# Start of a fused attention and MLP kernel: loads spread over two queues, and a new order of steps up to the third slot

## The chip, the cores and the metric

The kernel runs on one core of a Trainium2 chip. The core has a matrix engine (TensorE, in the profile PE, with its weight loads as PEld), a vector engine (VectorE, DVE), an engine for functions (ScalarE, ACT), a general engine (GpSimd, POOL) and an engine that mostly issues transfers (SyncE, SP). ScalarE can issue transfers too. All transfers are carried by 16 DMA engines. Each engine works through its own list of instructions in order, and waits where an operand isn't there yet.

The metric is the device time of one execution in microseconds (us). Before the change it was 173.32 us, the median of three runs (173.28 to 174.05).

## The reference

There are 2048 tokens of width 512. The result is the input, plus a linear attention of its layer norm, plus an MLP of the same layer norm. Cut to what matters (32 heads of 16):

```python
xn = layernorm(x)
q, k, v = split_heads(xn @ wqkv)
phi(t) = concat(softmax(t @ w_phi), softmax(-(t @ w_phi)))       # per head, 16 -> 32
kv = phi(k)^T @ v ;  z = sum over tokens of phi(k)
attn = (phi(q) @ kv) / (phi(q) . z + 1e-6) @ wo
h = xn @ w1 + b1                                                 # width 1792
mlp = (h * tanh(softplus(h))) @ w2                               # Mish
out = x + attn + mlp
```

## The kernel before, in words

Tokens lie in 16 tiles of 128, and four tiles form a group. A *slot* is a group whose keys (slots 0 to 3) or queries (slots 4 to 7) go through the feature map. The feature weights w_phi are folded into the key and query weights, so that a slot's logits come from one projection.

The order of the work is written out by hand in the table `STEPS`. Each entry is a step, and every engine gets its instructions in the order of the steps. `@` gives the PSUM bank (0 to 5) that a step writes. A letter at the end says who copies a result out of PSUM: `a` ScalarE, `v` VectorE. A step may write a bank only when its last content has been copied out. The steps that matter here:

- `AW n` is a dummy matmul of n columns, which keeps TensorE busy before there is data.
- `LS i`, `RS i`, `AZ i`: statistics of token tile i (VectorE), its reciprocal root (two tiny ScalarE instructions with `a`, two GpSimd ones with `p`), and the normalised tile (VectorE). `TP i @b` turns it on TensorE with four transposes, and `TC i` copies it out into `xnT`.
- The key weights `wkp` are needed turned for the fold. Half of them (row blocks 0 and 1) comes in naturally, is turned on TensorE (`TW kt`) and copied out (`TK kt`) into `wT`. The other half (row blocks 2 and 3) is turned by a transposing DMA. `WB` builds the block-diagonal feature weights `Wbd` from `wsrc`. `F0 kt` folds a row block with four matmuls, and `FD kt` copies it back into `wkp`.
- `LP` makes the logits of tiles 0 and 1 in eight matmuls (line 244). With `i` they alternate between the two tiles, one row block after the other.
- `V t` and `VC t`: values of a tile (four matmuls) and their copy. `L s i` and `LC s i`: logits of tile i of slot s (four matmuls) and their copy. `WL i` are logits of slot 1 that go to a wide PSUM tile. `H u` and `M u`: four matmuls of the first MLP layer, and Mish on ScalarE.
- `E s`, `X s k`, `S s k`, `R s k`, `N s k`, `A s k`: subtraction of extremes (VectorE), exponentials (ScalarE), sums (VectorE), reciprocals (ScalarE with `a`), normalisation (VectorE), accumulation into kv (TensorE, 16 matmuls).
- `LN g` and `AP g k`: statistics of a later group and its normalised halves, turned by DMA. `F`, `FC`, `FT`: the fold of the query weights. `PB` and `CB` bring the bias b1 into its layout.

ScalarE's functions lie in two table sets, one for Mish and one for exponential and logarithm. A step that needs the other set loads it first (line 139, `ACT_TABLE_LOAD`).

Nothing plans the order at run time: the table and the order of the loads (lines 517 to 533) set it. SP issues nearly all loads, ScalarE issues two small ones ahead of its first table load.

Of the kernel before, what the change touches and what calls it, by code (L numbers as in the profile page):

```python
# [59 lines left out]


# [1 line left out]
def kernel(  # L63
# [19 lines left out]
    FT = F // P  # L83
# [10 lines left out]
    b1_v = B_b1.rearrange("(f p) -> f p", p=P)  # L94
# [12 lines left out]
    x_sb = persist.tile([P, NT, D], BF16, name="x_sb")  # L107
# [118 lines left out]
    def project(w, t, pp):  # L226

        for kt in range(KT):
            nc.tensor.matmul(  # L229
                pp, lhsT=xnT[:, t, kt, :], rhs=w(kt),  # L230
                start=(kt == 0), stop=(kt == KT - 1),
            )
        return pp
# [292 lines left out]
    nc.scalar.dma_start(b1b[:], b1_v[:, :])  # L526
    with nc.allow_non_contiguous_dma(reason="tiny w_phi load"):
        nc.scalar.dma_start(wsrc[:], wphi_v)
# [191 lines left out]
```

## Time and profile before

| | |
|---|---|
| median of three runs | 173.32 us (173.28 to 174.05) |
| the profiled execution's own time | 173.45 us |
| its span in the profile | 171.7 us |
| PE busy | 166.9 us, 97% |
| DVE busy | 142.0 us, 83% |
| ACT busy | 124.4 us, 72% |
| HBM read and written | 7.10 MB and 2.10 MB |

The span is what lies between the first and the last instruction of the profiled execution. The 1.75 us around it belong to the execution's time. A row of the timeline gives the start and the length in us, the engine, the line, and what is written from what. `x8` means that eight instructions are merged, and in brackets stands how long the engine had been idle and what ended that. Instructions of VectorE and ScalarE overlap a little with the next one of the same engine, so the distance between two starts is often shorter than the length shown. A row of the windows gives the length of the stretch and then, engine by engine, busy time and count (PE, PEld, DVE, ACT, POOL), the granted clock of TensorE, the DMA engines' share and GB/s.

### The profile page before, as it was taken

How to read it: one execution, taken by the hardware profiler on the slowest of the kernel's cores; microseconds unless marked ns; L12 is line 12 of the kernel's file. 1: busy time of each engine (PE TensorE's matmuls, PEld its weight loads, DVE VectorE, ACT ScalarE, POOL GpSimd, SP SyncE). 2: the span in 40 equal slices, each digit the busy share in tenths (PEclk: the TensorE clock that was granted, in tenths of full speed). 3: DMA queues.
4: the chain of work that ended last, by engine and by line, in shares of the span. 5: the costliest groups of instructions: out<-in, count | busy, mean ns of one | idle time of the engine just before them, and what ended most of it. 6: DMA issues, size and time to landing. Idle time of an engine off the chain costs nothing.

```text
span 171.7 us, 2732 instructions
## 1 busy us (share of the span) xinstructions
PE 166.9 (97%) x1035; PEld 82.3 (48%) x1050; DVE 142.0 (83%) x221; ACT 124.4 (72%) x203; POOL 7.4 (4%) x21
## 2 busy tenths in 40 slices
PE   8899999999999999999999999999999999999993
PEld 3654444444444544454445644544444444554452
DVE  2968999989999999439989999899799998884333
ACT  3765999998999999799978989968272792432200
POOL 4021230200000000000000000000000000000000
PEclk9999999999999999999999999999999999999999
DMA  5997195184299100000000293309445628778741
GB/s 127 287 376 256 21 215 101 32 154 94 39 218 357 59 4 0 0 0 4 0 0 0 51 113 84 61 18 130 102 110 109 148 61 189 156 160 207 91 124 61
DMA packets 46297, 18.55 MB, mean 108 GB/s; under 512 B 38092, under 2 KB 46284, under 8 KB 46284
## 3 DMA queue, kind: packets, MB, share of 16 engines
q1 hardware_dynamic: 45584, 18.26, 46.4%
q10 hardware_dynamic: 700, 0.12, 0.4%
q8 instruction: 8, 0.13, 0.3%
q14 instruction: 5, 0.04, 0.1%
HBM read 7.10 MB, written 2.10 MB: 54 GB/s over the span
## 4 chain that ended last, share of the span: by engine, by line
PE 94%; DVE 2%; DMA 1%; issue 1%; ACT 0%
PE ph L263 28%; PE po L497 28%; PE pl L229 14%; PE pv L229 8%; PE po L504 8%; PE pnd L452 2%; PE pkv L421 2%; DMA x_sb<-in_A_x_dram 1%; PE pwide L229 1%; PE pl L244 1%; DVE stats L165 1%; PE ptr L609 1%; DVE wkp L160 0%; PE pfold L151 0%; DVE xn L176 0%
## 5 line engine op out<-in xcount | busy, mean ns | idle before, releaser
L497 PE MATMUL po<-w_sb,acts 128*128 128x512 bf16 (+2 forms) x232 | 50.2, 366 | 0.3
L263 PE MATMUL ph<-xnT,w_sb 128*128 128x512 bf16 x224 | 50.3, 379 | 0.0
L274 ACT ACTIVATE acts<-ph,b1f 128x512 bf16<-128x512 f32 x56 | 35.8, 698 | 3.1 <-PE ph L263 3.0
L340 DVE TENSOR_REDUCE s<-e 128x128 f32<-128x2048 bf16 x16 | 36.3, 2276 | 0.5 <-ACT e L323 0.5
L263 PEld LDWEIGHTS <-w_sb 128*128 128x128 bf16 x224 | 21.6, 98 | 25.7 <-issue 0.2
L497 PEld LDWEIGHTS <-acts 128*128 128x128 bf16 x238 | 22.1, 98 | 23.6
L323 ACT ACTIVATE e<-e 128x2048 bf16<-128x2048 bf16 x16 | 30.4, 1914 | 0.0
L229 PEld LDWEIGHTS <-xnT 128*128 128x128 bf16 x184 | 17.6, 98 | 20.4 <-issue 0.2
L287 ACT CAST p_sb<-pl 128x512 bf16<-128x512 f32 x26 | 14.8, 590 | 4.9 <-PE pl L229 4.8
L511 DVE TENSOR_TENSOR x_sb<-po,x_sb 128x512 bf16<-128x512 f32 (+2 forms) x17 | 11.0, 657 | 8.3 <-PE po L504 8.3
L229 PE MATMUL pl<-wqk,xnT 128*128 128x512 bf16 x64 | 15.6, 379 | 0.0
L229 PE MATMUL pv<-wv,xnT 128*128 128x512 bf16 x63 | 15.4, 379 | 0.1
L504 PE MATMUL po<-wqk,xnT 128*128 128x512 bf16 (+2 forms) x65 | 15.0, 366 | 0.2
L467 ACT COPY ds<-pnd 128x32 f32<-128x32 f32 x16 | 2.9, 183 | 16.5 <-PE pnd L452 16.5
L307 DVE TENSOR_TENSOR e<-p_sb,m 128x2048 bf16<-128x2048 bf16 x8 | 9.8, 1226 | 5.4 <-PE pkv L421 5.1
L165 DVE BATCH_NORM_STATS2 stats<-x_sb 128x6 f32<-128x512 bf16 x16 | 10.1, 680 | 4.3 <-DMA x_sb<-in_A_x_dram 4.3
L139 ACT ACT_TABLE_LOAD x10 | 12.8, 1283 | 0.2
L298 DVE TENSOR_TENSOR m<-m 128x512 bf16<-128x512 bf16 (+1 forms) x32 | 11.5, 359 | 1.1
L229 PE MATMUL pl<-wkp,xnT 128*128 128x512 bf16 x45 | 11.8, 379 | 0.2
L298 DVE TENSOR_TENSOR m<-p_sb 128x1024 bf16<-128x1024 bf16 x16 | 10.9, 682 | 0.3 <-ACT p_sb L287 0.3
L307 DVE TENSOR_TENSOR e<-m,p_sb 128x2048 bf16<-128x2048 bf16 x8 | 9.8, 1225 | 0.3
L374 DVE TENSOR_TENSOR e<-e,r 128x2048 bf16<-128x2048 bf16 x8 | 9.6, 1217 | 0.5 <-ACT r L349 0.5
(71 smaller groups left out, 129.0 us busy)
## 6 DMA issues: line engine op xcount, KB each, us to landing
w_sb<-in_B_w_dram SPq DMA_DIRECT2D x4, 896.0 KB, 8.3
out_dram<-x_sb SPq DMA_DIRECT2D x15, 128.0 KB, 1.9
x_sb<-in_A_x_dram SPq DMA_DIRECT2D x3, 512.0 KB, 8.2
wv<-in_A_wqkv_dram SPq DMA_DIRECT2D x1, 512.0 KB, 4.9
wqk<-in_A_wo_dram SPq DMA_DIRECT2D x1, 512.0 KB, 4.0
x_sb<-in_A_x_dram SPq DMA_DIRECT2D x2, 128.0 KB, 2.3
wkp<-in_A_wqkv_dram SPq DMA_DIRECT2D x1, 256.0 KB, 3.3
x_sb<-in_A_x_dram SPq DMA_DIRECT2D x1, 256.0 KB, 4.1
```

The lines of the kernel that those rows point to most:

```text
L139: nc.scalar.preload_act_table_set(name)
L165: nc.vector.bn_stats(stats[:, i, :], xs[:, i, :])
L229: nc.tensor.matmul(pp, lhsT=xnT[:, t, kt, :], rhs=w(kt), start=(kt == 0), stop=(kt == KT - 1),)
L263: nc.tensor.matmul(ph_of[u][:], lhsT=w1_sb[:, kt, f * P : (f + 1) * P], rhs=xnT[:, g * TPG : (g + 1) * TPG, kt, :], start=(kt == 0), stop= ...
L274: nc.scalar.activation(acts[:, f, g * 512 : (g + 1) * 512], ph_of.pop(u)[:], ACT.Mish, bias=b1f[:, f : f + 1])
L287: copy(p_of[s][:, i, :], pl_of.pop((s, i)))
L298: nc.vector.tensor_tensor(out=m[:], in0=src[:, :, 0:half], in1=src[:, :, half : 2 * half], op=op)
L307: nc.vector.tensor_tensor(out=e_of[s][:].rearrange("p t j l c -> p (t j) l c")[:, :, pl, :].rearrange("p t (c e o) -> p t c e o", e=8, o=2 ...
L323: nc.scalar.activation(v, v, ACT.Exp)
L340: nc.vector.reduce_sum(t[:], pair(s, k).rearrange("p t j l (c e) -> p (t j l c) e", e=16), axis=AX.X)
L497: nc.tensor.matmul(po_of[t, c.stop][:, c], lhsT=acts[:, f, t * P : (t + 1) * P], rhs=w2_sb[:, f, c], start=(f == 0), stop=False,)
L504: nc.tensor.matmul(po_of[t, c.stop][:, c], lhsT=oT_of[t // 2][:, t % 2 * 4 + j, :], rhs=wo_sb[:, j, c], start=False, stop=(j == 3),)
```

## The change

Five loads at the start are moved. SP keeps tile 0, then at once the transposing DMA of half of the key weights, tiles 2 and 3, and now the bias b1, ahead of the rest as before. ScalarE's queue gets the feature weights first, then the natural half of the key weights, then tile 1. Line numbers behind it fall by two.

The table `STEPS` is new from its start to the step `H 38` (logits of slots 0 to 3 and the first of slot 4), and from there on it is the same but for bank numbers. There are 13 dummies with 4480 columns in place of 15 with 4928. `WL 2` now comes ahead of `WL 1`, for which the allocation of the wide tile is made on first use.

```diff
-AW 256; AW 512; AW 128; AW 512; AW 256; AW 256; AW 512; AW 256; LS 0; AW 512; AW 512; LS 1; AW 256;
...
+AW 64; AW 512; LS 0; RS 0 a; AW 512; AW 128; AW 512; AW 512; AW 512; AZ 0; LS 1; AW 512; AW 512; AW
+256; AW 64; TW 0 @0; TW 1 @3; TK 0 a; WB v; TK 1 v; TP 0 @1; AW 256; RS 1 a; F0 0 @4; AZ 1; AW 128;
...
-    for t in range(2):
-        nc.sync.dma_start(x_sb[:, t, :], x_v[:, t, :])
-
-
+    nc.sync.dma_start(x_sb[:, 0, :], x_v[:, 0, :])
     wT_of = {0: lnp.tile([P, 4, 512], BF16, name="wT", tag="xn")}
-    nc.sync.dma_start(wkp[:, 0:2, :], wqkv_v[:, 0:2, D : 2 * D])
     nc.sync.dma_start_transpose(
         out=wT_of[0][:, :, 2 * P : 4 * P], in_=A_wqkv[2 * P : 4 * P, D : 2 * D]
     )
-    nc.scalar.dma_start(b1b[:], b1_v[:, :])
     with nc.allow_non_contiguous_dma(reason="tiny w_phi load"):
         nc.scalar.dma_start(wsrc[:], wphi_v)
+    nc.scalar.dma_start(wkp[:, 0:2, :], wqkv_v[:, 0:2, D : 2 * D])
+    nc.scalar.dma_start(x_sb[:, 1, :], x_v[:, 1, :])
     nc.sync.dma_start(x_sb[:, 2:4, :], x_v[:, 2:4, :])
+    nc.sync.dma_start(b1b[:], b1_v[:, :])
     nc.sync.dma_start(wv[:], wqkv_v[:, :, 2 * D : 3 * D])
...
     def wide(i):
-        if i == 1:
+        if not wide_of:
```

VectorE's list at the start, before. BN_STATS and BN_AGGR are a tile's statistics (`LS`), xn is a normalised tile (`AZ`), Wbd is `WB`, wT is `TK`, xnT is `TC`:

```order
L165 BN_STATS stats<-x_sb 128x6
L167 BN_AGGR mv<-stats 128x2
L165 BN_STATS stats<-x_sb 128x6
L167 BN_AGGR mv<-stats 128x2
L176 TENSOR_SCALAR xn<-x_sb,mv,rstd 128x512 x2
L565 TENSOR_TENSOR Wbd<-block,wsrc 128x512
L621 COPY wT<-ptw 128x4x128 x2
L668 CAST b1f<-pb 128x14
L627 COPY xnT<-ptr 128x512
L160 CAST wkp<-pfold 128x512
```

The same place now:

```order
L165 BN_STATS stats<-x_sb 128x6
L167 BN_AGGR mv<-stats 128x2
L176 TENSOR_SCALAR xn<-x_sb,mv,rstd 128x512
L165 BN_STATS stats<-x_sb 128x6
L167 BN_AGGR mv<-stats 128x2
L563 TENSOR_TENSOR Wbd<-block,wsrc 128x512
L619 COPY wT<-ptw 128x4x128
L176 TENSOR_SCALAR xn<-x_sb,mv,rstd 128x512
L625 COPY xnT<-ptr 128x512 x2
```

Tile 1's statistics moved behind tile 0's normalised tile, both copies to xnT moved to VectorE, and one wT copy and the fold's copy left it.

ScalarE's list at the start, before (rstd is `RS`, wkp from pfold is `FD`):

```order
L526 DMA b1b<-in_B_b_dram 14x128
L528 DMA wsrc<-in_A_w_phi_dram 128x4x16
L535 ACT_TABLE_LOAD
L594 ACTIVATE rstd<-mv,eps 128x1
L595 ACTIVATE rstd<-rstd 128x1
L594 ACTIVATE rstd<-mv,eps 128x1
L595 ACTIVATE rstd<-rstd 128x1
L627 COPY xnT<-ptr 128x512
L160 CAST wkp<-pfold 128x512 x3
```

The same place now:

```order
L523 DMA wsrc<-in_A_w_phi_dram 128x4x16
L524 DMA wkp<-in_A_wqkv_dram 128x2x512
L525 DMA x_sb<-in_A_x_dram 128x512
L533 ACT_TABLE_LOAD
L592 ACTIVATE rstd<-mv,eps 128x1
L593 ACTIVATE rstd<-rstd 128x1
L619 COPY wT<-ptw 128x4x128
L592 ACTIVATE rstd<-mv,eps 128x1
L593 ACTIVATE rstd<-rstd 128x1
L160 CAST wkp<-pfold 128x512 x4
```

Two large loads came in, tile 1's among them, a wT copy stands ahead of tile 1's root, and ScalarE makes all four copies of the fold.

ScalarE's list around the end of slot 0, before (acts are Mish, e is an exponential, s and r are the logarithm and the reciprocal, p_sb, pwide and vext are copies):

```order
L274 ACTIVATE acts<-ph,b1f 128x512 x13
L139 ACT_TABLE_LOAD
L323 ACTIVATE e<-e 128x2048 x2
L287 CAST p_sb<-pl 128x512
L139 ACT_TABLE_LOAD
L274 ACTIVATE acts<-ph,b1f 128x512 x6
L287 CAST p_sb<-pwide 128x512 x2
L274 ACTIVATE acts<-ph,b1f 128x512
```

The same place now:

```order
L139 ACT_TABLE_LOAD
L323 ACTIVATE e<-e 128x2048
L139 ACT_TABLE_LOAD
L274 ACTIVATE acts<-ph,b1f 128x512 x5
L139 ACT_TABLE_LOAD
L356 ACTIVATE s<-s 128x128
L349 ACTIVATE r_506<-s 128x256
L323 ACTIVATE e<-e 128x2048
L287 CAST p_sb<-pl 128x512 x2
L287 CAST p_sb<-pwide 128x512 x2
L253 CAST vext_104<-pv 128x8x64
L139 ACT_TABLE_LOAD
```

The two exponentials of slot 0 are now apart, with Mish between them, which brings two more table loads.

More of the change, by code (lines that the diff above doesn't have):

```diff
@@ new lines @@
+@5; M 12; M 1; AP 1 1; H 5 @4; M 9; DX 3; H 8 @3; LN 2; M 5; M 7; H 11 @5; M 8; E 0 1; L 1 0 @2; WL
+2; AP 2 0; M 11; L 1 3 @0; H 21 @5; H 22 @4; H 23 @1; LC 1 3 v; LC 1 0 a; X 0 0; H 17 @3; AP 2 1; M
+23; M 22; H 6 @0; WL 1; M 6; M 21; L 2 1 @4; M 17; LN 3; H 2 @1; S 0 0; L 2 0 @2; V 6 @0; LC 2 1 v;
+L 2 3 @3; AP 3 0; R 0 0 a; LC 2 0 v; AP 3 1; N 0 0; X 0 1; L 2 2 @5; V 3 @2; LC 2 3 a; LC 2 2 a; S 0
+1; LC 1 2 a; LC 1 1 a; H 26 @3; VC 6 a; H 15 @5; M 15; H 24 @4; H 18 @0; WT; H 19 @5; M 2; M 24; M
@@ new lines @@
+26; M 18; H 28 @1; M 28; F @3,4; FC 2 a; FC 3 a; H 29 @0; V 2 @1; H 16 @4; M 29; V 4 @3; H 14 @0; E
+1 0; FC 0 a; M 19; E 2 0; AM; E 1 1; FC 1 a; M 16; FT 0; VC 4 a; R 0 1 v; H 27 @4; VC 3 a; VC 2 a; M
+14; E 2 1; M 27; H 25 @2; H 20 @5; L 3 1 @1; M 25; M 20; L 3 2 @2; FT 1; V 9 @3; N 0 1; L 3 0 @5; X
+1 1; LC 3 2 v; LC 3 1 v; X 1 0; L 4 1 @0; A 0 0; L 3 3 @1; LC 3 0 a; S 1 1; H 32 @4; VC 9 a; X 2 0;
+V 5 @5; L 4 3 @2; S 1 0; LC 4 1 a; V 8 @3; R 1 1 a; V 11 @0; A 0 1; VC 8 a; L 4 2 @3; VC 5 a; LC 4 3
@@ new lines @@
+v; LC 3 3 a; R 1 0 a; S 2 0; H 33 @5; M 32; M 33; N 1 1; LC 4 2 a; VC 11 a; H 36 @2; L 4 0 @1; H 34
+@4; DW 3; V 7 @3; H 30 @5; LC 4 0 a; DW 2; VC 7 a; M 34; M 30; H 31 @3; H 35 @1; H 37 @0; M 31; M
+35; H 38 @4; E 3 0; H 39 @5; H 40 @3; M 36; N 1 0; M 37; M 38; M 39; H 41 @1; H 42 @2; H 43 @0; M
+40; A 1 0; M 41; E 3 1; M 42; M 43; A 1 1; X 2 1; V 12 @4; VC 12 a; L 5 0 @5; V 10 @3; V 15 @1; VC
+15 a; V 13 @2; V 14 @0; E 4 0; E 4 1; LC 5 0 a; VC 13 v; VC 10 a; L 5 2 @4; X 3 1; X 3 0; L 6 3 @1;
@@ new lines @@
+VC 14 a; L 5 3 @5; O 0 @2; LC 5 2 a; S 2 1; S 3 1; S 3 0; R 3 1 a; R 2 1 a; N 2 1; R 2 0 a; L 6 0
+@3; R 3 0 a; N 3 0; L 5 1 @0; LC 5 1 a; N 3 1; O 1 @4; L 6 1 @0; LC 6 0 a; LC 6 3 a; L 6 2 @3; H 44
+@1; X 4 0; N 2 0; S 4 0; LC 6 2 a; LC 6 1 v; LC 5 3 a; A 2 0; A 2 1; A 3 0; A 3 1; H 45 @3; X 4 1; M
+44; W 4 0 v; H 46 @5; H 47 @0; M 45; M 46; S 4 1; M 47; KV; H 48 @1; M 48; H 49 @3; H 50 @5; M 49; H
+51 @0; H 52 @1; M 50; M 51; Q 0 0; H 53 @3; G 0 0; H 54 @5; M 52; Q 0 1; H 55 @0; W 4 1 v; L 7 3 @1;
@@ new lines @@
+M 53; M 54; E 5 0; G 0 1; L 7 0 @3; E 5 1; Q 1 0; C 0 a; O 2 @5; G 1 0; LC 7 0 a; X 5 0; Q 1 1; O 3
+@3; G 1 1; E 6 0; S 5 0; P 0; P 1; C 1 a; LC 7 3 a; W 5 0 v; L 7 2 @1; M 55; Y 0; O 4 @0; O 5 @2; P
+2; LC 7 2 a; Y 1; X 5 1; Q 2 0; G 2 0; L 7 1 @4; E 6 1; LC 7 1 a; P 3; S 5 1; Y 2; W 5 1 v; X 6 0; Q
+2 1; G 2 1; O 6 @1; O 7 @5; E 7 0; C 2 a; S 6 0; Y 3; W 6 0 a; E 7 1; Q 3 0; O 8 @4; P 4; Y 4; G 3
+0; X 6 1; Q 3 1; G 3 1; X 7 0; S 6 1; C 3 a; O 9 @3; P 5; X 7 1; W 6 1 v; Q 4 0; G 4 0; O 10 @0; Y
@@ L59 @@
+5; Q 4 1; G 4 1; S 7 0; C 4 a; O 11 @2; W 7 0 v; Q 5 0; G 5 0; P 6; P 7; Q 5 1; G 5 1; Y 6; O 12 @1;
+S 7 1; C 5 a; Q 6 0; W 7 1 a; P 8; P 9; G 6 0; Q 6 1; Y 7; Y 8; Y 9; G 6 1; O 13 @5; Q 7 0; C 6 v; G
+7 0; P 10; P 11; Y 10; Q 7 1; O 14 @4; G 7 1; P 12; C 7 a; Y 11; Y 12; P 13; OH 0 @3; P 14; PH 0; OH
+1 @0; PH 1; Y 13; Y 14; YH 0; YH 1
 """
```

38 lines of the change are left out of this document (4 added, 34 removed).

## The prediction

> **What bounds the kernel now.** I read the page's shares first, then busy time by stages, then the timelines of the start, and last ScalarE's timeline from 24 to 60 us, which the new order rearranges. First the busy shares and two stages of PE.
>
> ```profile
> PE 166.9 (97%) x1035; PEld 82.3 (48%) x1050; DVE 142.0 (83%) x221; ACT 124.4 (72%) x203; POOL 7.4 (4%) x21
> ...
> 0.00:5.00 5.00, 3.98 (x15) 1.88 (x15) 1.85 (x5) 1.96 (x4) 1.79 (x13) 1.00 0.62 149
> 20.00:30.00 10.00, 9.95 (x47) 4.53 (x47) 9.86 (x25) 9.47 (x11) 1.68 (x2) 1.00 0.66 143
> ```
>
> From 20 us on PE has no gap (9.95 of 10 us), while VectorE (9.86) and ScalarE (9.47) are nearly full beside it. So whatever moves the first real matmuls moves the end one for one, and any new wait of PE is a loss that nothing gives back. The only thing to win lies ahead of about 9 us, where PE turns dummies (3.98 us in the first 5) and waits.
>
> The start, merged by engine: VectorE, ScalarE, PE.
>
> ```profile
> 3.08 0.69 DVE L165 BATCH_NORM_STATS2 stats<-x_sb 128x6 f32<-128x512 bf16 x1 [3.08 <-DMA x_sb<-in_A_x_dram]
> 3.81 0.18 DVE L167 BATCH_NORM_AGGREGATE mv<-stats 128x2 f32<-128x6 f32 x1
> ...
> 4.71 0.38 DVE L176 TENSOR_SCALAR xn<-x_sb,mv,rstd 128x512 bf16<-128x512 bf16 x1
> 5.39 0.41 DVE L176 TENSOR_SCALAR xn<-x_sb,mv,rstd 128x512 bf16<-128x512 bf16 x1 [0.30 <-ACT rstd L595]
> 5.72 0.42 DVE L565 TENSOR_TENSOR Wbd<-block,wsrc 128x512 bf16<-128x512 bf16 x1
> 6.05 0.75 DVE L621 COPY wT<-ptw 128x512 bf16<-128x512 bf16 x2
> ...
> 6.29 0.59 ACT L627 COPY xnT<-ptr 128x512 bf16<-128x512 bf16 x1 [0.94 <-PE ptr L609]
> ...
> 5.09 0.62 PE L616 MATMUL ptw<-ident,wkp 128*128 128x128 bf16 x8 [0.29 <-DMA wkp<-in_A_wqkv_dram]
> 5.86 0.40 PE L609 MATMUL ptr<-ident,xn 128*128 128x128 bf16 x4
> ...
> 7.59 1.90 PE L244 MATMUL pl<-wkp,xnT 128*128 128x512 bf16 x7
> 9.33 1.03 PE L229 MATMUL pv<-wv,xnT 128*128 128x512 bf16 x4
> ```
>
> The chain is tile 0's landing (3.08), then VectorE in order up to the wT copies (6.05), then fold and logits. The first logits (`LP`) run from 7.59 to 9.33 without a gap. What counts is when `LP` ends.
>
> **Part 1: when tile 1 lands.** The loads, by their issue and by their time to landing:
>
> ```profile
> 0.78 0.65 ACTq L526 DMA_DIRECT2D b1b<-in_B_b_dram  x1
> 1.46 0.41 ACTq L528 DMA_DIRECT2D wsrc<-in_A_w_phi_dram  x1
> 1.90 1.28 ACT L535 ACT_TABLE_LOAD   x1 [1.90 <-issue]
> ...
> wv<-in_A_wqkv_dram SPq DMA_DIRECT2D x1, 512.0 KB, 4.9
> ...
> x_sb<-in_A_x_dram SPq DMA_DIRECT2D x2, 128.0 KB, 2.3
> wkp<-in_A_wqkv_dram SPq DMA_DIRECT2D x1, 256.0 KB, 3.3
> x_sb<-in_A_x_dram SPq DMA_DIRECT2D x1, 256.0 KB, 4.1
> ...
> wsrc<-in_A_w_phi_dram ACTq DMA_DIRECT2D x1, 16.0 KB, 3.7
> ```
>
> ScalarE's queue now issues wsrc at 0.78 (0.65 for a queue's first), the key weights at 1.46 and tile 1 at about 1.9, where the table load starts today. The table load slides 0.4 us and still ends by 3.6, ahead of the first root at 4.1, so it costs nothing. Before, tile 1 was second on SP and landed 2.3 us after its issue. Now it is third, behind 16 KB in tiny packets and 256 KB, beside a transposing DMA on SP. Ends: 2.3 us gives 4.2; 4.9, as for wv, gives 6.8. I take wsrc's 3.7, between the key weights' 3.3 and the 4.1 of tiles 2 and 3, which also stood behind a large load: it lands at 5.6. The key weights land at 1.46 + 3.3 = 4.8, up to 5.6, and nothing on my chain needs them earlier.
>
> Every load of SP from tiles 2 and 3 on is issued some 0.4 us earlier (two issues of 0.44 less, b1 more), which hides under waits for other things; V 0 at 10 us finds wv long landed.
>
> **Part 2: the end of LP.** VectorE does tile 0's statistics at 3.08, its normalised tile at 4.71 (as today), and only then tile 1's statistics: at 5.04 at the earliest (0.33 behind, as from 5.39 to 5.72), at 5.6 with my landing. From there, with the distances of the rows above: statistics 0.91 (3.08 to 3.99), to 6.51; Wbd 6.52; wT copy 6.85; tile 1 normalised from 7.23 (the root takes 0.72, as from 3.99 to 4.71) to 7.64; transposes 7.69 (0.05 behind, as 5.80 to 5.86); copy 0.43 behind the start of the transposes (5.86 to 6.29), 8.12 to 8.53. The second matmul of LP is tile 1's and starts at 8.58; seven at 0.216 end at 10.09. The fold's four copies, now all on ScalarE, (0.59 each) start from 7.4 and are ready ahead of each turn. Against 9.33 this is **+0.76 us**; with tile 1 in time it is 9.53, +0.20, since VectorE's order alone already costs that.
>
> The dummies cost nothing: 832 columns fewer stand ahead of the first real matmul, which waits for its data either way, and the 256 and 128 columns put behind `TP 0` and the first fold lie in waits for Wbd and wT (0.16 us at full speed if those were gone). `PB`, one small matmul, moves from a wait to behind LP and adds **+0.05** (about a transpose's 0.06).
>
> **Part 3: the second pair of tiles.** Statistics of tiles 3 and 2 now come after tile 1's copy on VectorE.
>
> ```profile
> 9.41 0.18 DVE L167 BATCH_NORM_AGGREGATE mv<-stats 128x2 f32<-128x6 f32 x1
> ...
> 10.68 0.41 DVE L176 TENSOR_SCALAR xn<-x_sb,mv,rstd 128x512 bf16<-128x512 bf16 x1 [0.79 <-POOL rstd L172]
> ```
>
> Before, one V stood between the two transposes; now `TP 3` and `TP 2` follow each other behind one V. Tile 3: statistics from 8.47 to 9.38, root on GpSimd 1.09 (from 9.59 to 10.68), 10.47: in time for PE at 11.00. Tile 2: statistics to 10.29, root 0.72, 11.01, normalised to 11.42; PE has been through `TP 3` since 11.22 (four transposes, about 0.06 apart): **+0.2 us** (0 to 0.4).
>
> **Part 4: ScalarE from slot 1 to `V 7`.** Here the order is new and PE hangs on banks that ScalarE frees. Distances between its instructions:
>
> ```profile
> 32.15 3.58 ACT L274 ACTIVATE acts<-ph,b1f 128x512 bf16<-128x512 f32 x6
> 35.58 1.11 ACT L287 CAST p_sb<-pwide 128x512 bf16<-128x512 f32 x2
> ...
> 48.30 1.28 ACT L139 ACT_TABLE_LOAD   x1
> 49.60 1.91 ACT L323 ACTIVATE e<-e 128x2048 bf16<-128x2048 bf16 x1
> 51.41 0.57 ACT L287 CAST p_sb<-pl 128x512 bf16<-128x512 f32 x1
> 51.88 1.91 ACT L323 ACTIVATE e<-e 128x2048 bf16<-128x2048 bf16 x1
> ...
> 55.11 0.34 ACT L356 ACTIVATE s<-s 128x128 f32<-128x128 f32 x1
> ...
> 55.80 1.89 ACT L323 ACTIVATE e<-e 128x2048 bf16<-128x2048 bf16 x1
> ...
> 14.26 10.36 PE ph L263 x48
> 56.18 0.51 PE pkv L421 x16
> ```
>
> A Mish takes 0.572 ((35.58 - 32.15) / 6), a table load 1.30, an exponential 1.81, a copy 0.47, a logarithm with its reciprocal 0.69. In the new table ScalarE waits for `L 1 0`, and from its copy `LC 1 0` to `LC 4 2`, which frees bank 3 for `V 7`, it has 6 table loads (7.80), 5 exponentials (9.05), 20 Mish (11.44), 19 copies (8.93), 3 reciprocals (2.07), 0.7 for the ends of the instructions ahead of table loads, and `LC 4 2` itself 0.59: 40.6, with 0.2 for the two hand-overs 40.8 us. PE has between the end of `L 1 0` and `V 7` 45 groups of four matmuls at 0.863 (10.36 / 12), the fold of the queries, 0.4, and two accumulations at 0.51: 40.2 us. So PE waits **+0.6 us**, spread over `H 19`, `H 29`, `V 11`, `H 34` and `V 7`. Bounds: 1.5% off ScalarE's sum makes it nothing, 1.5% on makes it 1.2. The cause is the two table loads that the split exponentials of slot 0 bring (2.6 us), against four copies that go to VectorE.
>
> VectorE's extra copies (2.4 us) lie ahead of a long wait, so they cost nothing; without that cover they would delay slot 4:
>
> ```profile
> L307 DVE TENSOR_TENSOR e<-p_sb,m 128x2048 bf16<-128x2048 bf16 x8 | 9.8, 1226 | 5.4 <-PE pkv L421 5.1
> ```
>
> From `H 38` on, the steps are the same and move along with PE.
>
> **Sum.** 0.76 + 0.05 + 0.2 + 0.6 = 1.61 us on the profiled execution's 173.45 (span 171.7 and 1.75 around it): 175.06. That execution was 0.13 above the median of 173.32, so I forecast 174.9, +0.9%.
>
> **A rule weighed.** While wsrc came in on ScalarE's queue and the key weights on SP's, the two queues moved about equally many packets:
>
> ```profile
> q1 hardware_dynamic: 199, 0.18, 88.5%
> q10 hardware_dynamic: 184, 0.01, 17.2%
> ```
>
> This is the stretch from 3.6 to 4.2 us. Equal packets mean that a load of 1 KB packets on ScalarE's queue gets half the rate (0.19 MB in 0.6 us, so 0.16 of 0.32 MB/us) as soon as SP's queue carries 1 KB packets too: 0.39 MB from about 3.8 us on would take until 6.3, landing near 6.7. [...] By that rule, taken strictly, tile 1 would come 1.1 us later than I take and the sum would be 176.0; the row agrees with the rule, but SP's queue carries the small packets of the transposing DMA for part of the time.
>
> **Rivals.**
> 1. *Not slower: ScalarE keeps pace.* If its sum comes out at or below PE's 40.2 us less hand-overs (1.5% less than I sum), no bank is late and only the start counts: 0.45 us with tile 1 in time up to 1.0 with it at 5.6. 173.8 to 174.3, middle 174.0. For it: before, PE never waited for a bank; against: two more table loads.
> 2. *Tile 1 later still*, at 6.3 to 6.8, by the equal packets above: +0.7 to +1.2 on my sum, 175.6 to 176.1.
> 3. *TensorE's clock stays low.* The granted clock column says 1.00 throughout, but the dummies tell:
>
> ```profile
> 0.82 3.67 PE L554 MATMUL warm<-const-bfloat16-1.0 128*128 128x256 bf16 x12 [0.82 <-PEq L704]
> ```
>
> These 12 have 4224 columns, 0.87 ns each; the 48 matmuls of 512 at 14.26 take 0.42 ns per column. The last three (704 columns) end 0.31 us later, 0.44 ns: full speed came after some 3.6 us of unbroken work. Now 4096 columns, 3.4 us at that rate, precede a wait of about 0.6 us or more. If full speed then comes only after 3.6 us of work behind LP's start, some 1.6 us of columns take double: 176.5. [...]
> 4. *Faster by 0.9 us or more.* LP would have to end by 8.4, so tile 0 to land before 2.0 instead of 3.08, since VectorE's chain behind it takes 6.45 us (3.08 to 9.53) with everything else in time. It is issued at 0.79, and the shortest landing in the load rows is 2.3 us.
>
> **Chances.** A measurement of this kernel tells about 0.5% (0.87 us) from no change. Forecast 0.42; rival 1 0.23; rival 2 0.17; rival 3 0.13; rival 4 0.05. Rival 1 gives "same" 0.20 (its upper end touches slower), the forecast's low end 0.03; so faster 0.05, same 0.23, slower 0.72. The likeliest case spans 174.3 to 175.6. For 8 in 10 the range reaches to rival 1's middle below and to the clock above: 173.8 to 176.4.
>
> **What would show it.** Right: VectorE idle before tile 1's statistics until a DMA, near 5.6; the first values matmul at 10.1; a short wait before `TP 2`; PE waits of 0.1 to 0.3 us for ScalarE between 41 and 66 us; ScalarE without idle from 25 us to 66 us. Wrong: tile 1's statistics at 5.04, LP ending by 9.4, PE without waits behind 12 us, or matmuls of LP at twice their 0.216 us distance. The forecast fails above all if ScalarE's sum is off by a percent and a half or if tile 1 lands elsewhere.

## The result, and the profile after

The changed kernel takes **178.22 us** (median of four runs, 177.50 to 178.61) against 173.31 us for the kernel before in the same session (173.28 to 174.05): the ratio is **1.027** (95% interval 1.022 to 1.032). The forecast was 174.9 us with a range up to 176.4. The sign was right; the loss is three times as large as forecast, and outside the range.

The profiled execution took 177.88 us, 4.43 us more than the profiled one before (173.45). Its start, merged from the timelines of VectorE and PE, and the two accumulations of slot 1, behind which both kernels do the same:

```profile
5.04 0.63 PE L614 MATMUL ptw<-ident,wkp 128*128 128x128 bf16 x8 [0.64 <-DMA wkp<-in_A_wqkv_dram]
...
6.95 0.69 DVE L165 BATCH_NORM_STATS2 stats<-x_sb 128x6 f32<-128x512 bf16 x1 [1.98 <-DMA x_sb<-in_A_x_dram]
7.77 0.41 DVE L563 TENSOR_TENSOR Wbd<-block,wsrc 128x512 bf16<-128x512 bf16 x1
8.10 0.41 DVE L619 COPY wT<-ptw 128x512 bf16<-128x512 bf16 x1
8.23 0.38 PE L151 MATMUL pfold<-Wbd,wT 128*128 128x128 bf16 x4 [2.23 <-ACT rstd L592]
...
10.42 2.63 PE L244 MATMUL pl<-wkp,xnT 128*128 128x512 bf16 x7
12.99 0.18 PE L572 MATMUL pb<-ident,b1b 14*128 14x14 bf16 x1
13.10 1.04 PE L229 MATMUL pv<-wv,xnT 128*128 128x512 bf16 x4
...
78.83 1.18 PE L421 MATMUL pkv<-vext,e 128*128 128x65 bf16 x32
```

The row that answers to the last one in the kernel before:

```profile
74.41 1.18 PE L421 MATMUL pkv<-vext,e 128*128 128x65 bf16 x32
```

The reader is to see three things. VectorE stands idle for 1.98 us until tile 1 lands, at 6.95. `Wbd` and a wT copy come behind tile 1's statistics on VectorE, so PE, which needs `Wbd` for the first fold, waits 2.23 us. (The row puts that wait down to a ScalarE instruction that ended at the same moment; the operand is `Wbd`, ready at 8.18. The wT copy ends at 8.51 and serves the second fold.) And `LP`, whose row reads 1.90 us before, reads 2.63 (one of its eight matmuls is missing from either row; to the next start it is 1.74 and 2.57 us).

The first values matmul starts at 13.10 instead of 9.33, 3.77 us later. From there to the accumulations of slot 1 it was 65.08 us (9.33 to 74.41) and is 65.73 (13.10 to 78.83), 0.65 us more. The two make 4.42 of the 4.43 us.

The windows of one microsecond (columns as before; the granted clock is the third from the end) say why `LP` is slow:

```profile
8.00:9.00 1.00, 0.71 (x8) 0.60 (x8) 1.00 (x4) 0.74 (x3) 0.00 (x0) 0.75 1.12 373
9.00:10.00 1.00, 1.00 (x13) 1.00 (x11) 0.39 (x2) 0.82 (x2) 0.00 (x0) 0.50 1.03 373
10.00:11.00 1.00, 1.00 (x8) 0.72 (x7) 0.96 (x4) 0.76 (x2) 0.00 (x0) 0.50 1.04 373
11.00:12.00 1.00, 1.00 (x4) 0.29 (x2) 0.81 (x3) 0.43 (x2) 0.77 (x2) 0.54 1.10 356
```

0.75 in the first and 0.54 in the last mean half speed from 8.50 to 11.92 us, 3.41 us. In the trace the clock had risen at 5.09, 3.41 us before it fell.

The loads of the changed start, by their time from issue to landing, from the view of the transfers:

```profile
wkp<-in_A_wqkv_dram ACTq DMA_DIRECT2D x1, 256.0 KB, 3.7
x_sb<-in_A_x_dram SPq DMA_DIRECT2D x1, 256.0 KB, 5.1
...
x_sb<-in_A_x_dram ACTq DMA_DIRECT2D x1, 128.0 KB, 5.1
```

The first is the natural half of the key weights, the second tiles 2 and 3, the last tile 1. Tile 1 took 5.1 us to land, where it took 2.3 before and 3.7 was forecast.

### The profile page after: what moved, and what is told of

Same layout as the page of the kernel before. It is cut to its first block, busy times and chain, and to the rows that moved or that the text cites. A ratio compares the mean times of both kernels' runs of the same rounds, so it can differ in the third digit from the quotient of the medians.

```text
span 176.2 us, 2732 instructions
## 1 busy us (share of the span) xinstructions
PE 168.6 (96%) x1032; PEld 82.9 (47%) x1048; DVE 143.6 (82%) x223; ACT 126.1 (72%) x203; POOL 6.8 (4%) x21
## 4 chain that ended last, share of the span: by engine, by line
PE 81%; ACT 11%; DMA 3%; DVE 2%; issue 1%; ACTq 1%
PE po L497 27%; PE ph L263 22%; PE pl L229 11%; PE po L504 8%; PE pv L229 7%; ACT acts L274 3%; ACT L139 3%; DMA x_sb<-in_A_x_dram 3%; PE pnd L452 2%; PE pkv L421 2%; ACT e L323 2%; ACT p_sb L287 1%; DVE stats L165 1%; PE pfold L151 1%; PE ptr L607 1%
## 5 line engine op out<-in xcount | busy, mean ns | idle before, releaser
L263 PE MATMUL ph<-xnT,w_sb 128*128 128x512 bf16 x224 | 51.0, 379 | 0.2
L287 ACT CAST p_sb<-pl 128x512 bf16<-128x512 f32 x22 | 12.5, 588 | 3.8 <-PE pl L229 3.4
```

What stands on the lines that cost most here:

```text
L263: nc.tensor.matmul(ph_of[u][:], lhsT=w1_sb[:, kt, f * P : (f + 1) * P], rhs=xnT[:, g * TPG : (g + 1) * TPG, kt, :], start=(kt == 0), stop= ...
L287: copy(p_of[s][:, i, :], pl_of.pop((s, i)))
```

## The experiments

Two theories stood at the beginning. **Theory A**: the moved loads cost most; tile 1 lands late because its queue shares the DMA engines with the transposing transfer on SP's queue, VectorE's list holds back the fold's operands behind it, PE waits, and its clock falls. **Theory B**: the new order costs most, and the loads little.

### The loads or the order

`loads_alone` is the kernel before with only the new loads, `order_alone` the new table with the loads of before.

```diff
 # loads_alone, on the kernel before
-    for t in range(2):
-        nc.sync.dma_start(x_sb[:, t, :], x_v[:, t, :])
+    nc.sync.dma_start(x_sb[:, 0, :], x_v[:, 0, :])
...
+    nc.scalar.dma_start(wkp[:, 0:2, :], wqkv_v[:, 0:2, D : 2 * D])
+    nc.scalar.dma_start(x_sb[:, 1, :], x_v[:, 1, :])
 # order_alone: the changed STEPS, these lines as before
```

> The order of steps of before with the loads of after. Theory A: tile 1 lands near 6.9, and since VectorE's old list has tile 1's statistics even ahead of tile 0's normalised tile, the first logits end 5.4 us behind that (as 3.91 to 9.33 before), at 12.4, and up to 1.5 us later if the clock falls back: 176.4 to 178 us. Theory B: within 1 us of before, 173.3 to 174.3 us.

> The order of steps of after with the loads of before. Theory A: tile 1's statistics at 5.0, first logits end at 9.5, then the waits for ScalarE: 174.4 us (174.0 to 175.0), with PE's later waits as in the changed kernel. Theory B: above 176.5 us.

`loads_alone`: 178.79 us, ratio 1.030 (1.026 to 1.034), as slow as the whole change and slower than the 176.4 to 178 expected. `order_alone`: 174.65 us, ratio 1.007 (1.004 to 1.010). Tile 1's statistics, the first values matmul and the accumulations of slot 1 in `loads_alone`:

```profile
6.94 0.69 DVE L165 BATCH_NORM_STATS2 stats<-x_sb 128x6 f32<-128x512 bf16 x1 [2.99 <-DMA x_sb<-in_A_x_dram]
...
14.98 1.03 PE L229 MATMUL pv<-wv,xnT 128*128 128x512 bf16 x4
...
80.04 1.18 PE L421 MATMUL pkv<-vext,e 128*128 128x65 bf16 x32
```

and in `order_alone`:

```profile
4.90 0.69 DVE L165 BATCH_NORM_STATS2 stats<-x_sb 128x6 f32<-128x512 bf16 x1
...
9.62 0.18 PE L574 MATMUL pb<-ident,b1b 14*128 14x14 bf16 x1
9.73 1.04 PE L229 MATMUL pv<-wv,xnT 128*128 128x512 bf16 x4
...
75.43 1.18 PE L421 MATMUL pkv<-vext,e 128*128 128x65 bf16 x32
```

With the loads alone the start loses 5.65 us (14.98 against 9.33) and the middle nothing (65.06). The clock was at half speed there from 8.02 to 14.84 us, twice as long as in the changed kernel. With the order alone the start loses 0.40 and the middle 0.62 (65.70). Theory B falls: of the change's 2.7% the order accounts for 0.7. (The two parts do not add up to the whole, since what the late tile costs depends on the order behind it and on how long the clock stays low.)

### Why tile 1 is late

First, tile 1 back on SP's queue behind tile 0, all else as changed:

```diff
     nc.sync.dma_start(x_sb[:, 0, :], x_v[:, 0, :])
+    nc.sync.dma_start(x_sb[:, 1, :], x_v[:, 1, :])
...
-    nc.scalar.dma_start(x_sb[:, 1, :], x_v[:, 1, :])
```

> The changed kernel with one load put back: tile 1 goes out on SP right behind tile 0, ahead of the transposing DMA. Theory A (tile 1 comes late because it shares the DMA engines with the transposing DMA from another queue; VectorE's list then holds Wbd and the wT copy behind it, TensorE waits 2.2 us and its clock falls back): tile 1's statistics start at 5.0 instead of 6.95, the first logits end at about 9.6 instead of 13.0, the granted clock does not fall after its first rise, and what stays is the order's own price (0.25 at the start, up to 0.2 at the second pair of tiles, 0.65 from ScalarE): 174.4 us (173.9 to 174.9). Theory B (the new order of steps costs most, the loads little): stays above 176.5 us.

174.57 us, ratio 1.006 (1.004 to 1.008): this one line gives back 2.0 of the 2.7%. VectorE and PE:

```profile
4.91 0.69 DVE L165 BATCH_NORM_STATS2 stats<-x_sb 128x6 f32<-128x512 bf16 x1
...
9.53 0.18 PE L572 MATMUL pb<-ident,b1b 14*128 14x14 bf16 x1
```

So the place of tile 1 is the cause. Is it the transposing transfer beside it? Two kernels ask that: `plain_half` brings the second half of the key weights by a plain load, `turn_later` puts the transposing transfer behind tiles 2 and 3.

```diff
 # plain_half
-    nc.sync.dma_start_transpose(
-        out=wT_of[0][:, :, 2 * P : 4 * P], in_=A_wqkv[2 * P : 4 * P, D : 2 * D]
-    )
+    nc.sync.dma_start(
+        wT_of[0][:, :, 2 * P : 4 * P],
+        wqkv_v[:, 2, 0 : 2 * D].rearrange("p (j c) -> p j c", j=4),
+    )
 # turn_later: the transposing transfer moves behind this line
     nc.sync.dma_start(x_sb[:, 2:4, :], x_v[:, 2:4, :])
```

> The changed kernel, but the second half of the key weights comes in by a plain load of the same 256 KB (512-byte pieces, other rows of the weights, so the values that go into the fold differ). If it is the transposing transfer that slows the loads of ScalarE's queue, tile 1's statistics start at about 5.0 us, as with tile 1 on SP (4.91), LP ends by 9.7, no fall of the clock, and the time is 174.6 (174.2 to 175.2). If two queues share the engines' time whatever they carry, tile 1 still lands after 6.3 us and the time stays above 176.5.

> The changed kernel with the transposing transfer behind tiles 2 and 3 on SP. If it is the transposing transfer beside them that slows the loads, tile 1 lands by 5.0 to 5.6 us, PE's wait ahead of the first fold is gone, and the time is 174.5 to 175.3; the turned half then has to land by about 7.5 to cost nothing. If tile 1 is late because it stands third on ScalarE's queue, behind 16 KB in tiny packets and 256 KB, its statistics stay near 6.9 us and the time near 178.

178.70 us (ratio 1.030, 1.028 to 1.032) and 178.51 us (1.028, 1.027 to 1.030). In the first, and in the second, tile 1's statistics:

```profile
7.16 0.69 DVE L165 BATCH_NORM_STATS2 stats<-x_sb 128x6 f32<-128x512 bf16 x1 [1.94 <-DMA x_sb<-in_A_x_dram]
```

```profile
7.65 0.69 DVE L165 BATCH_NORM_STATS2 stats<-x_sb 128x6 f32<-128x512 bf16 x1 [2.65 <-DMA x_sb<-in_A_x_dram]
```

That part of theory A falls: tile 1 is late beside a plain load too, and later still beside tiles 2 and 3. The new theory was that two queues share the engines whatever they carry, and that the last of the 400 KB on ScalarE's queue is late. `tile1_ahead` exchanges tile 1 and the key weights on that queue:

```diff
-    nc.scalar.dma_start(wkp[:, 0:2, :], wqkv_v[:, 0:2, D : 2 * D])
     nc.scalar.dma_start(x_sb[:, 1, :], x_v[:, 1, :])
+    nc.scalar.dma_start(wkp[:, 0:2, :], wqkv_v[:, 0:2, D : 2 * D])
```

> The changed kernel with tile 1 ahead of the key weights on ScalarE's queue. New theory: tile 1 came late because two queues share the engines and 400 KB had to come in on its queue, whatever SP's queue carried. In the changed kernel 127 of that queue's 1 KB packets had started by 3.4 us, so tile 1, now the first 128, lands by 4.0 to 4.6 us and its statistics follow VectorE's own work at 5.0; the key weights take over the late place, 6.5 to 7.0 us, PE waits for them, and the time is 176 to 178. If it is something in tile 1's own load or in ScalarE's queue as such, its statistics still start after 5.5 us.

```profile
4.83 0.69 DVE L165 BATCH_NORM_STATS2 stats<-x_sb 128x6 f32<-128x512 bf16 x1
...
7.40 0.67 PE L614 MATMUL ptw<-ident,wkp 128*128 128x128 bf16 x8 [3.01 <-DMA wkp<-in_A_wqkv_dram]
```

Tile 1 is in time, the key weights take over the late place (7.40, 0.4 us later than expected), PE waits 3.01 us for them, and the time is 178.38 us, above the 178 expected. But is the last load late because SP's queue takes its share, or only because 272 KB stand ahead of it? `sp_behind` leaves ScalarE's queue as it is and holds back what SP issues behind tile 0, by letting GpSimd clear the place of the turned weights first; the transposing transfer and the loads behind it move below that line:

```diff
         nc.gpsimd.memset(vext[i][:, :, :, 64:66], 1.0)
+    nc.gpsimd.memset(wT_of[0][:, :, 2 * P : 4 * P], 0.0)
+    nc.sync.dma_start_transpose(
+        out=wT_of[0][:, :, 2 * P : 4 * P], in_=A_wqkv[2 * P : 4 * P, D : 2 * D]
+    )
+    nc.sync.dma_start(x_sb[:, 2:4, :], x_v[:, 2:4, :])
...
```

> The changed kernel in which SP's loads behind tile 0 are held back: GpSimd first clears the place of the turned weights, at 2.6 us and for a microsecond at most, and the transposing transfer, with all behind it, is issued after that, some 2 us later than in the changed kernel. ScalarE's queue and tile 1's place on it stay. If tile 1 is late because SP's queue takes its share of the engines, ScalarE's queue now has them alone for some 1.5 us and moves its 400 KB at about 0.29 MB/us: tile 1 lands by 4.9 and its statistics don't wait; LP ends by 10 unless the turned half, which would land at 7 to 8, holds the third fold, and the time is 174.5 to 175.8. If it is late because it stands third on its queue behind 272 KB whatever else moves, its statistics still start after 6 us and the time is 177 or more.

```profile
4.96 0.69 DVE L165 BATCH_NORM_STATS2 stats<-x_sb 128x6 f32<-128x512 bf16 x1
...
9.48 0.18 PE L574 MATMUL pb<-ident,b1b 14*128 14x14 bf16 x1
...
10.66 1.04 PE L229 MATMUL pv<-wv,xnT 128*128 128x512 bf16 x4 [1.00 <-DMA wv<-in_A_wqkv_dram]
```

Tile 1 is in time, third on its queue as before, and `LP` ends by 9.5 us. The time is 175.60 us (ratio 1.011, 1.008 to 1.014), 1.0 us above `tile1_on_sp`, because the held-back loads are now late themselves (PE waits 1.00 us for wv). What each queue moved from 3.0 to 4.4 us, in the changed kernel and in `sp_behind`:

```profile
q10 hardware_dynamic: 225, 0.22, 52.6%
q1 hardware_dynamic: 521, 0.13, 50.5%
```

```profile
q10 hardware_dynamic: 364, 0.34, 75.6%
```

q10 is ScalarE's queue (packets, MB, share of the engines' time). Alone it moved 0.34 MB where it moved 0.22 beside SP's queue. So sharing it is; neither the transposing transfer nor the place on the queue does it alone.

### What the late tile costs: the order of VectorE's list, and the clock

`weights_first` puts tile 1's statistics behind `Wbd` and the wT copy, so that these no longer wait for the tile:

```diff
-AZ 0; LS 1; AW 512; AW 512; AW 256; AW 64; TW 0 @0; TW 1 @3; TK 0 a; WB v; TK 1 v;
+AZ 0; AW 512; AW 512; AW 256; AW 64; TW 0 @0; TW 1 @3; TK 0 a; WB v; TK 1 v; LS 1;
```

> The changed kernel with VectorE's block-diagonal feature weights and wT copy put ahead of tile 1's statistics; the loads stay. Tile 1 still lands at 6.9 us. If the cost of the late tile is mostly that VectorE, which works in order, held these two back and so stopped PE, the folds start by 7 us, LP hangs on tile 1 alone and ends at about 11.4 us where the changed kernel ended at 13.0 (statistics 0.91, root 0.72, normalised 0.41, transposes, copy, seven matmuls at full clock): 176.3 us (175.9 to 176.8). If only the landing counts, or if PE's wait, which moves behind the second fold and is still some 1.7 us long, lowers the clock just the same, 177.3 or more.

Its runs took 176.22, 177.99 and 178.94 us (the ratio, 1.020, 1.016 to 1.024, is of the first two alone; a fourth, of 456 us, was disturbed and is left out): the two outcomes expected both occur. The mean granted clocks of the three go the same way: 0.999, 0.990 and 0.981. In the profiled execution (178.94) the first fold came at 6.16 us, 2.1 us earlier, and PE then waited for tile 1 instead:

```profile
6.16 0.40 PE L151 MATMUL pfold<-Wbd,wT 128*128 128x128 bf16 x4
...
8.96 0.61 PE L607 MATMUL ptr<-ident,xn 128*128 128x128 bf16 x4 [1.91 <-DVE xn L176]
```

There the clock fell at 7.64 us and stayed down until 14.46, and the gain was gone. Two kernels take the clock by itself: `dummies_in_wait` has the ten dummies of 512 columns behind `TP 0` that the diff shows, and `filled_both` also the two ahead of `TW 0`, so that both of PE's waits are filled.

```diff
-AW 256; AW 64; TW 0 @0; TW 1 @3; TK 0 a; WB v; TK 1 v; TP 0 @1; AW 256; RS 1 a;
+AW 256; AW 64; AW 512; AW 512; TW 0 @0; TW 1 @3; TK 0 a; WB v; TK 1 v; TP 0 @1; AW 256;
+AW 512; AW 512; AW 512; AW 512; AW 512; AW 512; AW 512; AW 512; AW 512; AW 512; RS 1 a;
```

> The changed kernel with ten more dummies of 512 columns behind the first tile's transposes, where TensorE waits from 6.0 to 8.2 us; nothing else is touched. If the clock falls back because TensorE stands still there, the granted clock stays at full from 5.1 us on, the first logits end near 11.5 instead of 13.0 and the time is 176.4 us (176.0 to 176.9). If the first logits are slow for another reason (the copies of the fold, the loads), the time stays at 177.9 us or above.

> The changed kernel with dummies of 512 columns in both of PE's waits: two ahead of the first transposes of the weights, ten ahead of the first fold; the loads and the late tile 1 stay. If the low clock is what separates the 178 us from the sum, LP ends at 11.4 us and all runs lie at 176.2 to 176.9 (173.45 + 2.11 at the start + 0.05 + 0.65 in the middle is 176.3), without runs at 178. If the clock has no share, the dummies change nothing: 177.5 to 178.6.

`dummies_in_wait`: four runs from 176.48 to 176.88 us and two at 178.4 (ratio 1.018, 1.016 to 1.021). The profiled one was of the two: the clock rose only at 9.63 us, and the dummies themselves, at half speed, held up the fold until 10.24. `filled_both`: 176.70 us, all four runs from 176.49 to 177.06 (ratio 1.019, 1.017 to 1.021), 1.5 us less than the changed kernel, with tile 1 as late as before:

```profile
7.10 0.69 DVE L166 BATCH_NORM_STATS2 stats<-x_sb 128x6 f32<-128x512 bf16 x1 [2.08 <-DMA x_sb<-in_A_x_dram]
...
9.83 1.92 PE L245 MATMUL pl<-wkp,xnT 128*128 128x512 bf16 x8
11.68 0.18 PE L573 MATMUL pb<-ident,b1b 14*128 14x14 bf16 x1
```

The clock's share is 1.5 us. When the clock rises differs from profile to profile (3.48 to 9.63 us in these kernels), and the runs of some of them lie in two groups some 1.5 us apart. That the groups are early and late rises is likely, but a trace is kept of one execution of each kernel only. It bears on the changed kernel too: its two slowest executions (178.56 and 178.61 us) have mean granted clocks of 0.999 and 0.998, without the fall that gave the profiled one 0.989. A late first rise would explain them, since the column reads 1.00 ahead of it (in `dummies_in_wait` too, where 512 columns took 0.43 us until 9.63); that is not shown.

### The middle

The forecast put 0.6 us there and named two more table loads of ScalarE as the cause. The stretch from the first values matmul to the accumulations of slot 1 (two of the expectations call them slot 2's) tells of it. Three kernels, all with the new order and the loads of before. `exp_together` moves slot 0's first exponential next to the second, which saves both table loads; `identity_exp` instead leaves that exponential out (an activation of the same shape without a table stands there); `no_exp` leaves out slot 1's two exponentials as well, with slot 1's subtraction turned round.

```diff
 # exp_together
-LC 1 0 a; X 0 0; H 17 @3;
+LC 1 0 a; H 17 @3;
...
-H 2 @1; S 0 0; L 2 0 @2;
+H 2 @1; L 2 0 @2;
...
-R 0 0 a; LC 2 0 v; AP 3 1; N 0 0; X 0 1;
+LC 2 0 v; AP 3 1; X 0 0; X 0 1;
...
-LC 2 2 a; S 0 1;
+LC 2 2 a; S 0 0; R 0 0 v; N 0 0; S 0 1;
 # identity_exp and no_exp
+        if (s, k) == (0, 0):
+            nc.scalar.activation(v, v, ACT.Identity, scale=-1.0)
+            return
         table("natural_log_exp_and_others")
 # no_exp
-        nc.scalar.activation(v, v, ACT.Exp)
+        if s != 1:
+            nc.scalar.activation(v, v, ACT.Exp)
```

> The new order with the loads of before, and slot 0's first exponential moved next to the second, its reciprocal to VectorE: ScalarE has two table loads (2.6 us) and 0.69 us of reciprocal less between the logits of slot 1 and the values of tile 7. If these table loads are the cost of the new order in the middle, the stretch from the first values matmul to the last accumulation of slot 1 falls from 65.70 to 65.1 us and the time is 174.1 (ratio 1.003). If it is something else in the order (which copies are whose, which bank), the stretch stays at 65.6 to 65.8 and the ratio at 1.007.

> The new order with the loads of before, but slot 0's first exponential is left out: an activation of the same shape that needs no table stands in its place (sign turned, so the attention comes out otherwise). ScalarE's list is the same but for two table loads (2.6 us), and all else keeps its place. If these table loads are what the new order costs in the middle, the stretch from the first values matmul to the two accumulations of slot 2 falls from 65.70 to 65.1 us, PE's waits between 40 and 60 us are gone, and the time is 174.0 (ratio 1.003). If ScalarE isn't the bound there, the stretch stays at 65.6 to 65.8.

> As the new order with the loads of before and slot 0's first exponential left out (no table, two table loads fewer), and now slot 1's two exponentials (3.7 us of ScalarE at 53 to 57 us) are left out as well; the subtraction of slot 1 is turned round so that the sums stay positive. If all of PE's waits in the middle hang on ScalarE's load, the three behind 57 us (0.03, 0.18 and 0.13) go too, and the stretch from the first values matmul to the accumulations of slot 2 falls from 65.47 to 65.1 us. If they hang on the places of the copies in the order, it stays at 65.4 to 65.5.

`exp_together` was a miss: 178.85 us (median of six; the ratio, 1.027, 1.024 to 1.031, is without the slowest). In its profiled execution the clock was late again (the first values matmul came at 10.98 us), and the stretch became 68.5 us instead of the 65.1 expected, because the reciprocal and the sums that I moved along held up VectorE, and PE waited for a copy of VectorE's:

```profile
59.98 1.02 PE L229 MATMUL pl<-wkp,xnT 128*128 128x512 bf16 x3 [2.03 <-DVE p_sb L287]
```

It says nothing on the table loads, since it exchanged one loaded engine for another.

`identity_exp` does. Its profiled execution took 174.24 us, and the stretch ran from 9.71 to 75.18, 65.47 us. PE's longest gap of `order_alone` there (two matmuls 0.47 us apart at 41 us, where 0.22 is usual) is gone, the others are unchanged: leaving two table loads out is worth 0.23 us, not the 0.6 expected. Most of the 2.6 us that they take never reached PE, because ScalarE then stood idle between 25 and 32 us, three times and 2.3 us in all. The longest:

```profile
29.36 1.26 ACT L274 ACTIVATE acts<-ph,b1f 128x512 bf16<-128x512 f32 x2 [1.41 <-PE ph L263]
```

(All its runs: median 175.56, ratio 1.011, 1.007 to 1.014. They lie in two groups, 174.2 to 174.3 and 175.5 to 176.0, and the profiled one is of the first.) `no_exp`: 174.01 us (ratio 1.004, 1.002 to 1.007), and the stretch:

```profile
9.79 1.04 PE L229 MATMUL pv<-wv,xnT 128*128 128x512 bf16 x4
...
74.92 1.18 PE L425 MATMUL pkv<-vext,e 128*128 128x65 bf16 x32
```

65.13 us, as before the change (65.08) and as the first theory expected. So the 0.62 us hang on ScalarE's load: its windows from 40 to 70 us in the changed kernel are full (9.97, 9.97 and 9.91 of 10, the fourth busy column), and where it has 3.7 us less to do, PE's waits behind 57 us go. A full ScalarE alone is not enough, though: in the kernel before, the same column reads 9.87, 9.94 and 9.56 without the loss. What else in the order has to come to it is not shown.

```profile
40.00:50.00 10.00, 9.79 (x59) 4.24 (x58) 9.60 (x15) 9.97 (x18) 0.00 (x0) 1.00 0.41 81
50.00:60.00 10.00, 9.95 (x60) 4.81 (x60) 9.46 (x14) 9.97 (x13) 0.00 (x0) 1.00 0.82 217
60.00:70.00 10.00, 9.92 (x60) 4.61 (x59) 9.79 (x11) 9.91 (x18) 0.00 (x0) 1.00 0.23 73
```

### A version meant to beat both

`both_copies` is the kernel before with the feature weights issued first on ScalarE's queue, `Wbd` in VectorE's gap between the two normalised tiles, one wT copy on each engine, and the first fold ahead of tile 0's transposes:

```diff
-AZ 0; RS 1 a; AZ 1; TW 1 @0; TP 1 @2; PB @1; TP 0 @5; TC 1 a; WB v; TK 0 v; TK 1 v; F0 0 @4; CB;
+AZ 0; WB v; RS 1 a; AZ 1; TW 1 @0; TK 0 a; TK 1 v; TP 1 @2; F0 0 @4; TC 1 a; TP 0 @5; PB @1;
```

> The kernel before with three things at the start: the feature weights issued ahead of the bias on ScalarE's queue, the block-diagonal weights made in VectorE's gap between the two normalised tiles, and the first wT copy on ScalarE beside the second on VectorE, with the first fold ahead of tile 0's transposes. The first fold can start at 6.2 us (transposes of the weights at 5.09, copies 0.43 and 0.65 behind), 0.3 us earlier than before (6.53), and with it LP. If the fold chain bounds LP's start, LP starts at 7.25 to 7.4 and the time is 173.0 to 173.2 where before has 173.35 to 173.5 (ratio 0.998). If the normalised tiles bound it, nothing changes (ratio 1.000).

```profile
6.28 0.40 PE L151 MATMUL pfold<-Wbd,wT 128*128 128x128 bf16 x4
...
7.72 1.89 PE L244 MATMUL pl<-wkp,xnT 128*128 128x512 bf16 x8
```

174.06 us, ratio 1.004 (1.002 to 1.005): not faster. The first fold came 0.25 us earlier, but `LP` at 7.72 instead of 7.59, since PE has no gap left between the two: transposes, bias and the other twelve fold matmuls fill it. No version here beats the kernel before.

## Why the prediction was wrong, point by point

**Part 1, when tile 1 lands: the step that failed.** Taken 5.6, with ends 4.2 and 6.8; measured 6.95. The value came from wsrc's 3.7 us, the landing of 16 KB, while tile 1 was the last of 400 KB on its queue; the right row would have been the sharing of the two queues, which stood in the prediction as a rule weighed (6.7) and as rival 2 (0.17). That its 6.7 came so near is partly luck: it let the 0.39 MB start at 3.8 us at 0.16 MB/us, and ScalarE's queue moved 0.40 MB from 2.45 to 6.2, 0.11 MB/us. Nor were the packets that the profile counts shared equally (330 to 163 in `plain_half`, last section). By Part 2's own distances the landing costs 1.35 us more than forecast (6.95 - 5.6).

**Rival 3, the clock, came with it.** The sum had no term for it. It was priced at about 1.6 us and given 0.13 as a case by itself. Measured: 1.5 us, by two ways. By Part 2's working `LP` ends 4.49 us behind tile 1's statistics (5.6 to 10.09), so at 11.44; it ended at 12.99, 1.55 later. And `filled_both`, which keeps the clock up, is 1.5 us faster. The mistake was to treat rivals 2 and 3 as alternatives: the late tile made the wait (2.23 us), and behind the wait the clock fell (to 0.50 at 8.50). The places of the cause were named; that they are one chain was missed, and the range, which let neither be added to the other, was too short by 1.8 us. The reason given was also off: the clock had risen before the wait and fell after it.

**Part 2** otherwise held. The distances from tile 1 to `LP`'s end are right wherever the clock was up: tile 1's statistics at 7.10 and `LP`'s end at 11.68 in `filled_both` (4.58 for 4.49), 9.53 in `tile1_on_sp` where 9.53 was forecast for tile 1 in time. `PB` took 0.11 instead of 0.05.

**Part 3, +0.2 us before `TP 2`: wrong, nothing was lost.** No wait stands there, neither in the changed kernel, where `LP` was late, nor in `order_alone`: its values start at 9.73 and the next ones 1.32 us later, which is four values matmuls (0.87) and eight transposes (0.45). VectorE had both tiles in time.

**Part 4, +0.6 us in the middle: right in size, and mostly in place.** Measured +0.65 (and +0.62 in `order_alone`, whose waits stand at `H 19`, `V 11` and `V 7`, three of the five steps named). ScalarE needed 40.86 us from `LC 1 0` (28.43) to the end of `LC 4 2` (68.70 and 0.59), 40.6 were summed. The cause was named too narrowly: the two table loads are worth 0.23, and the rest went when slot 1's exponentials went. A sum of ScalarE's work over the whole stretch takes all of it as alike, but what was saved early was mostly lost again while ScalarE waited for PE (0.23 of 2.6 us stayed).

**The sum.** 1.61 forecast; with 1.35 for the landing, 1.55 for the clock, 0.06 for `PB`, 0.05 in the middle and -0.2 for Part 3 it is 4.42, against 4.43 measured.

**The clock's step.** In the trace of the changed kernel the clock was up at 5.09, down at 8.50 and up at 11.92, 3.41 us from one to the next. It fell after a wait of 2.23 us. Rival 3's 3.6 us of unbroken work were read from the kernel before alone; in the changed kernel the rise came 0.70 us behind the end of the dummies (0.82 to 4.39), in `identity_exp` after 2.66 us of them.

## What to carry to other kernels

Here a second DMA queue added no bandwidth (249 GB/s from 3.0 to 4.4 us with both at work, 244 in `sp_behind` with ScalarE's alone): it redistributed it, and what stood last on the queue with the most urgent bytes paid. Work out the landing of a load from all bytes that move beside it, not from a landing of like size. And put no instruction that another engine waits for behind a late operand on an in-order engine: here `Wbd` behind tile 1's statistics made PE wait 2.23 us, and the clock that fell behind that wait cost 1.5 us more, so two rivals that follow from each other belong into one sum.

## What the runs showed of the hardware that was not expected

**The clock fell after windows that were partly busy.** The traces give PE's busy time in the 3.41 us behind each rise. Three of them, of the changed kernel, `weights_first` and `order_alone`:

```profile
5.09:8.50 3.41, 1.18 (x18) 1.04 (x18) 1.52 (x5) 1.08 (x3) 0.00 (x0) 1.00 1.12 285
```

```profile
4.22:7.64 3.42, 1.95 (x24) 1.27 (x22) 1.83 (x4) 0.92 (x3) 0.00 (x0) 1.00 1.18 206
```

```profile
3.93:7.34 3.41, 2.33 (x30) 1.67 (x29) 2.58 (x7) 2.18 (x7) 0.00 (x0) 1.00 1.05 281
```

After 1.18 and 1.95 us of 3.41 the clock fell, after 2.33 it stayed; in `identity_exp` it stayed after 2.14. In these runs the border lay between 57% and 63%. Once down, the clock stayed down after windows of that length with 2.51 and 2.57 us busy (`loads_alone`, `plain_half`), and it rose after 2.66 (`identity_exp`, 0.07 to 3.48).

**The two queues did not share by the packets that the profile counts.** In `plain_half`, from 3.0 to 4.4 us, SP's queue (512-byte packets) and ScalarE's (1 KB) moved the same bytes in unequal numbers of packets:

```profile
q1 hardware_dynamic: 330, 0.17, 40.4%
q10 hardware_dynamic: 163, 0.17, 39.8%
```

Beside the transposing transfer, from 4.5 to 6.0 us in the changed kernel, it was neither:

```profile
DMA packets 576, 0.22 MB, mean 146 GB/s; under 512 B 477, under 2 KB 576, under 8 KB 576
...
q1 hardware_dynamic: 491, 0.14, 79.7%
q10 hardware_dynamic: 85, 0.08, 40.4%
```

All engines together moved 146 GB/s there. In the kernel before, while the same transfer ran with SP's queue nearly alone (4.2 to 5.2 us), it was 279:

```profile
DMA packets 1093, 0.28 MB, mean 279 GB/s; under 512 B 1060, under 2 KB 1093, under 8 KB 1093
```

The packets counted in `plain_half` are of 512 bytes and 1 KB (0.17 MB in 330 and in 163), and these did not go in turn one for one. Why the rate was about half beside the transposing transfer in the changed kernel (146 for 279 GB/s), the runs do not tell.
